# A block's transposes at the end of its group, its value products one group later: chunked attention feeding two feed-forward layers

## The chip, the cores and the metric

The kernel runs on one core of a Trainium2 chip. The metric is the device time of one execution in microseconds (us): the median of three runs of the kernel before was 1510.13 us (1508.39 to 1510.74). The engines are TensorE (PE; its weight loads are listed as PEld), VectorE (DVE), ScalarE (ACT), GpSimd (POOL) and SyncE (SP), which issues every DMA of this kernel. Nothing reorders the program: each engine's instructions stand in the order in which the kernel issues them.

## The reference, cut to what matters

```
# attention in chunks of 64 positions; q, k, v: (8, 8, 576, 64)
scores = 1/sqrt(64) * q_c @ k_c^T            # per chunk, 64 x 64
attn   = exp(scores - max) / (sum + 1e-9)
x      = attn @ v_c                          # then laid out as (4608 tokens, 512)
# first feed-forward layer, d_ff = 2048
h = x @ w_in ;  g = h * cos(h) ;  x = g @ w_out
# second layer, d_ff = 1024
out = (((x @ w1) * (x @ w2)) @ w3) @ w_out2
```

Every matrix product in fp32 is made of three products of high and low parts (`mm3`, L104 to L108), so operands are split into a high part (an ACT copy) and a low part (a DVE or POOL subtraction).

## The kernel before, in words

The 4608 tokens are 9 tiles of 512. The 2048 columns of the first layer are 8 groups of 256. The work of the first layer is done in two passes over the tiles: the first pass takes groups 0 to 4 of every tile (45 steps of the loop, `groups`, called groups below), the second pass groups 5 to 7. After that comes the second layer. This case is about the first pass.

Within a group the order is written out by hand as a string, one letter for one piece of work (`ORDER0`, `ORDER1P`, `ORDER1`, and the ones with an E at the end for the fifth group of a tile, which has no attention in it). Every engine gets its instructions in the order of the letters. The letters that matter here:

- `P`, `Q` (tiles 0 and 1) or `1`, `2`, `5`, `3` (later tiles): the input product x @ w_in into PSUM banks `ps_hh`. P's result is d, Q's is e. In the later tiles DVE adds the parts up (d at L489 and L501, e at L499 and L508).
- `a`, `c` (an ACT copy to integers, L547), `A`, `C` (DVE, L552), `b`, `d` (on ACT: Abs at L557, a table load, Sin at L558), `B`, `D` (DVE, L562): g = h * cos(h), the first letter of each pair for d and the second for e. In tiles 0 and 1 the PSUM bank of P is free again only when B has read it.
- `s`: the split of the previous group's g (ACT L570, POOL L571). `x`, `y`: the two halves of the previous group's output product g @ w_out into the four banks `acc` (12 matmuls each). At the first group of a tile `y` is followed by the copies of `acc` (L593, L595).
- `v` (tile 0): one step of the conversion of weights from HBM (`conv_tick`: ACT L124 and L177, DVE L125, L126, L132 and L199, and DMAs of SP). `l`, `m`, `h`, `r` and `M`, `H`, `R` (later tiles): the same kind of work, for weights that are staged in HBM.
- `o`, `S`, `T` (the fifth group): the split of the attention output xf into the operands X of the next tile (ACT L101, DVE L102).
- `q`: the next of the five attention steps of one block of 128 positions; there is one block in each of the first four groups of a tile, for the tile after. Step A is the scores (PE L361 into two banks `ps_s`; DVE L367 and L369; then the loads of q and k for a later block, SP L339 and L340). B is Exp (ACT L375, with a table load). E is the sums and the scaling (DVE L380 to L383, then POOL L384). C is the transposes (four matmuls, PE L391 into one bank `ps_at`, then the copy `pt` on ACT, L393). D is the values (32 small matmuls, PE L404 into two banks `ps_v`; the load of the next block's v, SP L345, into the one buffer `vt`; then two ACT copies into xf, L409).

The banks of `ps_s`, `ps_at` and `ps_v` are two that are given out in turn; `ex` and `pt` share two buffers; the banks `ps_hh` are two.

In the strings the five `q` of a group are A, B, E, C, D in this order. In tile 0 C stands behind `D` and one `v` ahead of the values, so the values end the group. In the later tiles C stands between `x` and `y`, and the values behind `y`.

Of the kernel before, what the change touches and what calls it, by code (L numbers as in the profile page):

```python
# [21 lines left out]
NJ = NT // P  # L22
# [4 lines left out]
FB2 = 8  # L27
# [6 lines left out]

START = "A0 A1 x B0 E0 B1 C0 x E1 A2 D0 C1 x B2 E2 A3 D1 C2 o o B3 E3 D2 C3 x D3 o o"

ORDER0 = "PsvaAqQvqcCqxybBdvDqvq"
ORDER0E = "PsvaAQvcCxybBodDoooL"
ORDER1P = "PsqMhQqqHaclAxqbCrRmBdyqDL"
ORDER1PE = "SPsQacATCoobBoxodoDyoo"  # L40
ORDER1 = "1s2qMh5qqHa3clAxqbCrRmBdyqDL"
ORDER1E = "S1s25a3cATCoobBoxodoDyoo"
ORDER2 = "1s2h5a3clAxbCrdByDm"
ORDER3 = "12sqhlrmq5a3cAbCdBDxy"
# [3 lines left out]
FOLD = 1  # L48
# [8 lines left out]
def chunk_attention_two_ffn(  # L57
# [38 lines left out]
    def f32(ap):  # L96
        return ap.bitcast(F32)
# [137 lines left out]
    def need(*keys):  # L235
        while not all(key in W for key in keys):
            assert (pump() if cat[3] == len(cq) else conv_tick()), keys
# [66 lines left out]
    def pump():  # L304

        n = 0
        while lq:
            key = lq[0]
            kept = (("w12", key[0][1] % FB2), key[1]) if key[0][0] == "w12" else key
            if kept not in staged or (kept != key or key[0][0] == "w12") and key[0][1] > unit[0] + AHEAD:  # L310
                break
            if key[1] == 3 and isinstance(key[0], tuple):
                if not free(s4s, 1):
                    break
                t = new_s4(key)
            elif free(slots, 1):
                t = new_w(key)
            else:
                break
            nc.sync.dma_start(out=f32(t), in_=staged[kept])  # L320
            lq.pop(0)
            n += 1
        return n
# [89 lines left out]
    def att_tok(step, early):  # L413
        (att_scores, att_softmax, att_scale, att_transpose, att_values)["ABECD".index(step[0])](int(step[1:]), early)
# [145 lines left out]
    def chain_g(i, h, which):  # L560
        t = rr[i, which]
        nc.vector.tensor_tensor(out=t, in0=t, in1=h, op=ALU.mult)  # L562
# [193 lines left out]
    with tc.manual_schedule():  # L756
# [17 lines left out]

        def order_of(i, nth, end):
            if i < GA:
                return ORDER0E if end else ORDER0
            if i < 2 * GA:
                return ORDER1PE if end else ORDER1P
            if i <= iA:  # L780
                return ORDER1E if end else ORDER1
            if i < iB:
                return ORDER2
            return (ORDER3X if nxt in xs else ORDER3E) if end else ORDER3B if nth else ORDER3

        steps = [s + str(j) for j in range(4, NJ) for s in "ABECD"]
        NG = len(groups)
        iA, iB = (NTILE - 1) * GA, NTILE * GA
        n_sums = 0
        fq = 0  # L790
        for i in range(NG):
            if i == GA:
                sq.extend(("wo2", j) for j in range(FB2))
                for g in range(GA, G1):
                    sq.extend((nm, 2 * g + e) for nm in ("in", "out") for e in range(2))
                    lq.extend((("in", g), p_) for p_ in range(4))
                    lq.extend(("out", 2 * g + e) for e in range(2))
                lq.extend(("wo2", j) for j in range(FB2))
                sq.extend(("w3", j) for j in range(N3))
                for f in range(FB2):  # L800
                    sq.extend((nm, f) for nm in ("w1", "w2"))
                    if N3 + f < 16:
                        sq.append(("w3", N3 + f))
                lq.extend((("w12", u), p_) for u in range(UNITS) for p_ in range(4))
                st_load()
            if i == iB + FOLD - 1:
                load_w3()
                load_w3()
            ps, n, g = groups[i]
            k_tile = (i - iB) // (G1 - GA)  # L810
            nxt = PASS2[k_tile + 1] if 0 <= k_tile < NTILE - 1 else None
            nth = (g, g - GA)[ps]
            end = g == (GA, G1)[ps] - 1

            def load_x(op):
                if op in pre:
                    X[op], pre[op] = pre[op], X[op]
                else:
                    nc.sync.dma_start(out=f32(X[op]), in_=xs[nxt][op])

            need(*((("in", g), p_) for p_ in range(2 if i < 2 * GA else 4)))
            z = Plain(("in", g)) if i < 2 * GA else Seven(
                ("in", g), (bank_h,) * 4, False, load_x if ps and end and nxt in xs else None)
            if i:
                need(*(("out", 2 * groups[i - 1][2] + e) for e in range(2)))
            n_q = n_o = 0
            for op in order_of(i, nth, end):
                if op == "s" and i:
                    split_g(i - 1)
                elif op == "x" and i:  # L830
                    x2_mm(i - 1, 0)
                elif op == "y" and i:
                    x2_mm(i - 1, 1)
                elif op == "v":
                    conv_tick()
                elif op == "L":
                    if n_sums < GA:
                        sum_load(n_sums)
                        n_sums += 1
                elif op == "M":  # L840
                    if loaded and i > GA + loaded[0][0]:
                        sum_make()
                elif op in "HR":
                    if sp:
                        {"H": sum_hi, "R": sum_lo}[op]()
                elif op == "l":
                    st_low()
                elif op == "m":
                    st_bits()
                elif op == "h":  # L850
                    st_hi()
                elif op == "r":
                    st_lo()
                elif op in "1253PQ":
                    getattr(z, "step" + op)()
                elif op in "ac":
                    chain_t(i, z.d if op == "a" else z.e, "ac".index(op))
                elif op in "AC":
                    chain_r(i, z.d if op == "A" else z.e, "AC".index(op))
                elif op in "bd":  # L860
                    chain_cos(i, "bd".index(op))
                elif op in "BD":
                    chain_g(i, z.d if op == "B" else z.e, "BD".index(op))
                elif op == "q":
                    if i < iA and nth < 4:
                        att_tok(steps[20 * n + 5 * nth + n_q], False)
                    elif i >= iB + FOLD and fq < 4 * FB2:
                        need(("w3", fq // 2), *(("wo2", j) for j in range(FB2)))
                        fold(fq // 4, fq % 4)
                        fq += 1  # L870
                        if fq == 4 * FB2:
                            load_wf(0)
                            load_wf(1)
                    n_q += 1
                elif op in "ST":
                    x_sums("ST".index(op))
                elif op == "o":
                    if i < GA and not n_o:
                        x_plain()
                    x_op((z.done if i < GA or i >= 2 * GA else OPS)[n_o], n + 1 if ps == 0 else None)  # L880
                    n_o += 1
            if i >= iA:
                pump()
            if n == (NTILE - 1, PASS2[-1])[ps]:
                done_with((("in", g), p_) for p_ in range(4))
            if ps == 1:
                if nth == 0 and nxt in xs:
                    if not pre:
                        xr = one.tile([P, CC, TT], F32R, tag="xf", name="xr")
                        pre.update((op, xr[:, 2 * j:2 * j + 2]) for j, op in enumerate(("B11", "B21")))  # L890
                    for op in pre:
                        nc.sync.dma_start(out=f32(pre[op]), in_=xs[nxt][op])
                if nth == 0 and nxt not in xs:
                    if pre:
                        pre.clear()
                        xf = one.tile([P, CC, TT], F32, tag="xf", name="xf")
                    nc.sync.dma_start(out=xf, in_=x2d[ALONE] if nxt is None else xd[nxt])
                if end:
                    for c in range(CC):
                        load_x2a(n, c)  # L900
        need(*(("out", 2 * G1 - 2 + e) for e in range(2)))
        assert fq == 4 * FB2 and sat[1] == len(sq) and not now
        split_g(NG - 1)
        for f in (4, 5, 6):
# [39 lines left out]
        j = FB2  # L944
# [75 lines left out]
```

## Time and profile before

| | |
|---|---|
| median of 3 runs | 1510.13 us (1508.39 to 1510.74) |
| profiled execution: time, and span of its instructions | 1515.81 us, 1514.0 us |
| PE busy | 1455.7 us, 96% of the span |
| DVE busy | 1099.8 us, 73% |
| ACT busy | 766.9 us, 51% |
| POOL busy | 262.0 us, 17% |
| first pass, tile 0 (groups 0 to 4) | about 34 to 115 us in the span |
| first pass, tile 1 | about 115 to 184 us |
| first pass, tiles 2 to 7 (attention still in them) | about 184 to 566 us |

A share is an average over stages; matmuls overlap, so a busy PE need not be at its peak. In the timelines below the number in front is the start in us from the beginning of the span, then the duration, the engine, the line, and in brackets the idle time ahead of the instruction with what ended it.

### The profile page before, as it was taken

The numbers are of one execution on the slowest core, as the hardware profiler recorded it, in microseconds if no ns is written. First come the engines' busy times: TensorE is split into PE (matmuls) and PEld (weight loads), VectorE is DVE, ScalarE is ACT, GpSimd is POOL, SyncE is SP. The second block draws the span as 40 slices with busy tenths as digits, with TensorE's granted clock in tenths as the row PEclk, the third lists the DMA queues.
The fourth block names the chain that finished last, engine by engine and source line by source line (L and its number), as shares of the span: only waits on it lengthen the run. The fifth ranks groups of instructions, "written<-read, shape, count | busy, mean of one in ns | idle before, by whom it ended". The sixth has DMA issues, their size and how long they took to land.

```text
span 1514.0 us, 26149 instructions
## 1 busy us (share of the span) xinstructions
PE 1455.7 (96%) x9996; PEld 1251.1 (83%) x9996; DVE 1099.8 (73%) x1844; ACT 766.9 (51%) x1317; POOL 262.0 (17%) x194
## 2 busy tenths in 40 slices
PE   4789999999999999999999989999999999999998
PEld 4678778888888888888888878898888888888886
DVE  6986798888988887767777777776665656656553
ACT  3777788888888876555555555321122013004002
POOL 0222222222222222222222112120100200200000
PEclk9999999999999999999999999999999999999999
DMA  7664555565665626998889774596434542641501
GB/s 235 204 210 133 188 173 204 188 228 166 227 218 165 229 88 248 363 328 299 309 308 326 252 282 127 196 367 238 152 140 154 190 153 90 228 157 59 210 33 56
DMA packets 122814, 307.39 MB, mean 203 GB/s; under 512 B 13633, under 2 KB 25665, under 8 KB 121537
## 3 DMA queue, kind: packets, MB, share of 16 engines
q1 hardware_dynamic: 122688, 305.71, 58.3%
q8 instruction: 79, 1.29, 0.4%
q14 instruction: 47, 0.38, 0.1%
HBM read 210.50 MB, written 95.16 MB: 202 GB/s over the span
## 4 chain that ended last, share of the span: by engine, by line
PE 65%; ACT 12%; DVE 12%; DMA 7%; issue 2%; POOL 1%; SPq 0%; DVEq 0%; ACTq 0%; POOLq 0%
PE ps_hh L106 9%; PE acc L107 8%; PE acc L106 8%; PE acc L108 8%; PE ps_hh L108 8%; PE ps_hh L107 8%; PE ps_aa L107 4%; PE ps_aa L106 4%; PE ps_aa L108 4%; ACT t L558 2%; DMA sd<-raw 2%; ACT L375 2%; ACT t L557 2%; ACT L558 1%; POOL ex L384 1%
## 5 line engine op out<-in xcount | busy, mean ns | idle before, releaser
L571 POOL TENSOR_TENSOR g<-t,g 128x512 fp32r<-128x512 f32 x144 | 196.2, 1384 | 591.6 <-ACT g L570 517.2
L106 PE MATMUL acc<-g,w 128*128 128x512 f32 x576 | 228.6, 397 | 0.0
L107 PE MATMUL acc<-g,w 128*128 128x512 f32 x576 | 227.1, 394 | 0.1
L108 PE MATMUL acc<-g,w 128*128 128x512 f32 x576 | 225.0, 391 | 0.0
L108 PE MATMUL ps_hh<-T,w 128*128 128x256 f32 (+1 forms) x616 | 182.2, 296 | 6.3 <-DVE w L199 6.2
L106 PE MATMUL ps_hh<-T,w 128*128 128x256 f32 (+1 forms) x616 | 185.3, 301 | 0.5 <-ACT x L481 0.5
L107 PE MATMUL ps_hh<-T,w 128*128 128x256 f32 (+1 forms) x616 | 181.8, 295 | 0.0
L108 PEld LDWEIGHTS acc<-g,w 128*128 128x128 f32 x576 | 108.5, 188 | 23.3
L107 PEld LDWEIGHTS acc<-g,w 128*128 128x128 f32 x576 | 108.9, 189 | 22.3 <-POOL g L571 3.0
L108 PEld LDWEIGHTS ps_hh<-T,w 128*128 128x128 f32 x616 | 118.6, 193 | 9.4 <-DVE w L199 6.9
L106 PE MATMUL ps_hh<-B,w 128*128 128x256 f32 (+1 forms) x396 | 120.4, 304 | 5.3 <-DVE t L562 3.3
L106 PEld LDWEIGHTS acc<-g,w 128*128 128x128 f32 x576 | 108.9, 189 | 19.7
L106 PEld LDWEIGHTS ps_hh<-T,w 128*128 128x128 f32 x616 | 118.6, 192 | 6.4 <-ACT x L481 0.9
L745 ACT ACTIVATE phl<-e 128x512 fp32r<-128x512 f32 x32 | 20.2, 633 | 201.5 <-DVE e L743 201.5
L107 PEld LDWEIGHTS ps_hh<-T,w 128*128 128x128 f32 x616 | 118.6, 193 | 3.2
L107 PE MATMUL ps_hh<-B,w 128*128 128x256 f32 (+1 forms) x396 | 116.6, 294 | 0.0
L108 PE MATMUL ps_hh<-B,w 128*128 128x256 f32 (+1 forms) x396 | 116.4, 294 | 0.0
L558 ACT ACTIVATE t<-t,half_pi 128x512 f32<-128x512 f32 x144 | 104.3, 724 | 4.0
L106 PE MATMUL acc<-wf,phl 128*128 128x512 f32 x252 | 98.2, 390 | 1.5 <-DVE o L688 1.5
L107 PE MATMUL acc<-wf,phl 128*128 128x512 f32 x252 | 98.1, 389 | 0.0
L108 PE MATMUL acc<-wf,phl 128*128 128x512 f32 x252 | 98.0, 389 | 0.0
L547 ACT ACTIVATE t<-d 128x512 int32<-128x512 f32 x62 | 38.9, 628 | 115.8 <-DVE d L501 115.8
(200 smaller groups left out, 3513.8 us busy)
## 6 DMA issues: line engine op xcount, KB each, us to landing
w<-sd SPq DMA_DIRECT2D x159, 512.0 KB, 5.6
sd<-raw SPq DMA_DIRECT2D x104, 256.0 KB, 4.5
s<-sd SPq DMA_DIRECT2D x43, 256.0 KB, 4.8
qk<-in_q_dram SPq DMA_DIRECT2D x36, 256.0 KB, 4.4
qk<-in_k_dram SPq DMA_DIRECT2D x36, 256.0 KB, 4.5
vt<-in_v_dram SPq DMA_DIRECT2D x72, 128.0 KB, 3.1
x2a<-x2o SPq DMA_DIRECT2D x36, 256.0 KB, 2.6
x2a<-x2a SPq DMA_DIRECT2D x36, 256.0 KB, 6.0
```

What stands on the lines that cost most here:

```text
L106: nc.tensor.matmul(ps, a[0], b[0], start=first, stop=False)
L107: nc.tensor.matmul(ps, a[0], b[1], start=False, stop=False)
L108: nc.tensor.matmul(ps, a[1], b[0], start=False, stop=last)
L375: nc.scalar.activation(ex, ex, AF.Exp, scale=SCALE)
L384: (nc.vector if early else nc.gpsimd).tensor_tensor(out=ex, in0=ex, in1=rc.unsqueeze(2).to_broadcast([P, 2 * HP, 64]), op=ALU.mult)
L547: nc.scalar.activation(t.bitcast(I32), h, AF.Copy, scale=INV2PI)
L557: nc.scalar.activation(t, t, AF.Abs)
L558: nc.scalar.activation(t, t, AF.Sin, scale=-TWO_PI, bias=half_pi)
L571: nc.gpsimd.tensor_tensor(out=lo, in0=r, in1=f32(hi), op=ALU.subtract)
L745: nc.scalar.activation(t[:, 0], e0, AF.Copy)
```

## The change

The five `q` are replaced by a digit for each step: `6` scores, `7` Exp, `8` sums and scaling, `9` transposes, `0` values, each with a counter of blocks of its own, so that a step can stand in another group than the one before it. Scores, Exp and scaling stay where they were.

- Tile 0: the transposes `9` stay behind `D`. The values `0` of a block move into the next group, between `x` and `y`. The first group has no values, and the fifth group (`ORDER0E`) has the last block's.
- Tiles 1 to 7: in the first three groups the transposes move from between `x` and `y` to the end, behind `y`. The values move to the next group, ahead of `x`. The fourth group has the third block's values ahead of `x`, its own transposes between `x` and `y`, and its own values behind `y`.

The load of v (L345) and the copies into xf (L409) move with the values, the copy `pt` (L393) with the transposes. Nothing is added or taken out, and no buffer or bank changes.

```
-ORDER0 = "PsvaAqQvqcCqxybBdvDqvq"
-ORDER0E = "PsvaAQvcCxybBodDoooL"
-ORDER1P = "PsqMhQqqHaclAxqbCrRmBdyqDL"
+ORDER0 = ("PsvaA6Qv7cC8xybBdvD9v",) + 3 * ("PsvaA6Qv7cC8x0ybBdvD9v",)
+ORDER0E = "PsvaAQvcCx0ybBodDoooL"
+ORDER1P = ("Ps6MhQ78HaclAxbCrRmBdy9DL",) + 2 * ("Ps6MhQ78HaclA0xbCrRmBdy9DL",) + ("Ps6MhQ78HaclA0x9bCrRmBdy0DL",)
 ORDER1PE = "SPsQacATCoobBoxodoDyoo"
-ORDER1 = "1s2qMh5qqHa3clAxqbCrRmBdyqDL"
+ORDER1 = ("1s26Mh578Ha3clAxbCrRmBdy9DL",) + 2 * ("1s26Mh578Ha3clA0xbCrRmBdy9DL",) + ("1s26Mh578Ha3clA0x9bCrRmBdy0DL",)
 ORDER1E = "S1s25a3cATCoobBoxodoDyoo"
...
             if i < GA:
-                return ORDER0E if end else ORDER0
+                return ORDER0E if end else ORDER0[nth]
             if i < 2 * GA:
-                return ORDER1PE if end else ORDER1P
+                return ORDER1PE if end else ORDER1P[nth]
             if i <= iA:
-                return ORDER1E if end else ORDER1
+                return "".join(o for o in ORDER1[0] if o not in "67890") if i >= iA and not end else ORDER1E if end else ORDER1[nth]
...
-        steps = [s + str(j) for j in range(4, NJ) for s in "ABECD"]
+        at_block = {s: 4 for s in "67890"}
...
+                elif op in at_block:
+                    att_tok("ABECD"["67890".index(op)] + str(at_block[op]), False)
+                    at_block[op] += 1
                 elif op == "q":
-                    if i < iA and nth < 4:
-                        att_tok(steps[20 * n + 5 * nth + n_q], False)
-                    elif i >= iB + FOLD and fq < 4 * FB2:
+                    if i >= iB + FOLD and fq < 4 * FB2:
```

## Rows read from the trace of the kernel before

**Rows 1.** Waits of PE, 44 to 560 us: total, times, longest
```profile
PE ps_at L391 <- POOL ex L384: 9.0, 13, 4.2
PE ps_hh L108 <- DVE w L199: 6.2, 2, 3.1
PE ps_hh L106 <- DVE t L562: 3.3, 4, 0.9
PE ps_v L404 <- ACT pt L393: 3.0, 4, 0.8
```

**Rows 2.** Busy time by stretch: length, engines, PE clock granted, DMA share
```profile
71.00:78.00 7.00, 7.00 (x76) 6.42 (x76) 6.93 (x15) 5.55 (x8) 0.00 (x0) 1.00 0.65 213
103.60:107.00 3.40, 3.06 (x14) 3.07 (x15) 1.48 (x3) 0.47 (x1) 0.00 (x0) 0.50 0.96 323
```

**Rows 3.** Timeline of PE, tile 0 and the start of tile 1
```profile
57.76 0.40 PE L106 MATMUL acc<-g,w 128*128 128x512 f32 x1
...
65.00 0.79 PE L404 MATMUL ps_v<-pt,vt 64*64 64x64 f32 x32 [0.78 <-ACT pt L393]
...
75.76 0.40 PE L106 MATMUL acc<-g,w 128*128 128x512 f32 x1
...
90.20 0.40 PE L106 MATMUL acc<-g,w 128*128 128x512 f32 x1
...
109.46 0.40 PE L106 MATMUL acc<-g,w 128*128 128x512 f32 x1
...
114.93 0.28 PE L106 MATMUL ps_hh<-B,w 128*128 128x256 f32 x1
...
117.89 0.69 PE L361 MATMUL ps_s<-qk 64*64 64x64 f32 x32
```

**Rows 4.** Timeline of ACT, tile 0
```profile
59.45 0.62 ACT L557 ACTIVATE t<-t 128x512 f32<-128x512 f32 x1
...
65.94 0.63 ACT L409 ACTIVATE xf<-ps_v 128x256 f32<-128x256 f32 x2
...
110.21 0.62 ACT L557 ACTIVATE t<-t 128x512 f32<-128x512 f32 x1
...
114.34 0.61 ACT L101 ACTIVATE B<-xf 128x512 fp32r<-128x512 f32 x1
```

**Rows 5.** Timeline of DVE, tile 0
```profile
62.22 0.64 DVE L562 TENSOR_TENSOR t<-t,ps_hh 128x512 f32<-128x512 f32 x1
62.78 1.29 DVE L132 CUSTOM_DVE_ANT_0 cw<-raw,cw 128x1024 uint16<-128x1024 uint16 x1
...
66.25 0.68 DVE L132 CUSTOM_DVE_ANT_0 cw<-raw,cw 128x1024 uint16<-128x1024 uint16 x1
...
79.20 0.69 DVE L562 TENSOR_TENSOR t<-t,ps_hh 128x512 f32<-128x512 f32 x1 [0.34 <-ACT t L558]
...
95.37 0.64 DVE L562 TENSOR_TENSOR t<-t,ps_hh 128x512 f32<-128x512 f32 x1
```

**Rows 6.** Timeline of ACT and DVE, first group of tile 1
```profile
124.88 0.60 ACT L393 ACTIVATE pt<-ps_at 128x512 f32<-128x512 f32 x1 [1.96 <-PE ps_at L391]
125.37 0.62 ACT L557 ACTIVATE t<-t 128x512 f32<-128x512 f32 x1
...
128.06 0.69 DVE L562 TENSOR_TENSOR t<-t,ps_hh 128x512 f32<-128x512 f32 x1 [3.10 <-ACT t L558]
```

**Rows 7.** Timeline of ACT and DVE, a group of tile 2
```profile
222.34 0.68 ACT L253 ACTIVATE raw<-raw 128x512 int32<-128x512 uint32 x1
223.09 0.60 ACT L393 ACTIVATE pt<-ps_at 128x512 f32<-128x512 f32 x1
223.59 0.62 ACT L557 ACTIVATE t<-t 128x512 f32<-128x512 f32 x1
...
228.87 0.69 DVE L489 TENSOR_TENSOR d<-x,ps_hh 128x512 f32<-128x512 f32 x1 [0.62 <-ACT g L570]
```

**Rows 8.** Transfers of `vt`, 183 to 560 us
```profile
DMA to landing us min/median/max: 2.6/3.1/5.3
```

More of the change, by code (lines that the diff above doesn't have):

```diff
@@ L901, in chunk_attention_two_ffn @@
         need(*(("out", 2 * G1 - 2 + e) for e in range(2)))
+        assert set(at_block.values()) == {NJ}
         assert fq == 4 * FB2 and sat[1] == len(sq) and not now
```

## The prediction

> **What bounds the kernel now.** I read the share of each engine first: TensorE is busy 96% of the span, so its waits look like the prize. Then its waits over the first pass [rows 1]: 9.0 us in 13 waits of the transposes for GpSimd's scaling, 3.0 us in 4 waits of the values for ScalarE's copy `pt`, 3.3 us of P for B, and 6.2 us in two waits of P for a converted weight (L199). The first two lie beside the steps that move. Then the busy time by stretch: in tile 0 VectorE is busy 6.93 of 7.00 us [rows 2], because it converts weights there. So TensorE's waits in tile 0 are a symptom, VectorE sets its length, and whatever makes VectorE idle there adds to the end. Last, the timelines of single groups, to see what stands in line behind each moved instruction on its own engine.
>
> 0.2% of 1510.13 is 3.0 us, about what a measurement of this kernel can tell from no change.
>
> **Tile 0: the copies into xf now stand ahead of the cosine.** Before, ScalarE goes from the copy to integers straight to Abs (`b`), and the two copies into xf come last in the group. Now they are issued between `c` and `b`, and they need the values, which TensorE takes up only after `x`. ScalarE's order is the program's, so Abs, the table load, Sin, and VectorE's B behind them wait for TensorE to finish `x` and the values. `x` is half of the 24 matmuls from 109.46 to 114.93, that is 2.74 us [rows 3]; from the start of the values (65.00) to the copies (65.94) it is 0.94 [rows 3, 4]; the pair of copies takes 0.63, and the next instruction starts 0.10 before the end of the one ahead, as at 223.59 [rows 7]: 0.53. Abs can start 2.74 + 0.94 + 0.53 = 4.21 us after Q's end. From Abs to B it is 62.22 - 59.45 = 2.77 [rows 4, 5].
>
> - Second group: Q ends at 57.76, so B at 64.74 instead of 62.22: 2.5 late. VectorE did something useful up to 62.22 (no idle is shown), so this is idle time. Given back: L132 took 1.29 behind B and takes 0.68 elsewhere [rows 5]; the late one no longer meets GpSimd's scaling, 0.6. The values no longer hold up P at the end of the first group: about 0.5, an estimate from their 0.79. Net 1.4.
> - Third group: Q ends at 75.76, B at 82.74 instead of 79.20, 3.5; with the 0.1 that is left of L132, 3.4. Q shifts with VectorE, since P waits for L199.
> - Fourth: Q ends at 90.20, B at 97.18 instead of 95.37, 1.8, less 0.6 for L132 as in the second (an estimate): 1.2.
> - Fifth: Q ends at 109.46, Abs at 113.67 instead of 110.21, 3.5 late, and the four splits of X for the next tile hang behind it. The last ACT part starts at 114.34 now, so at 117.8 then and ends at 118.4; its low part on VectorE follows that of the split before it, done about 119.4. The last quarter of P (2.96 us from 114.93 to 117.89) then ends at 120.3 instead of 117.9: 2.4 late, `x`, values and `y` included.
>
> Sum for tile 0: 1.4 + 3.4 + 1.2 + 2.4 = 8.4 us lost. The cover for a late B would be VectorE work that is ready ahead of it; there is none in program order. Bounds: 0 if such cover existed, and 2.5 + 3.5 + 1.8 + 3.5 = 11.3 with nothing given back.
>
> **Tensor clock.** TensorE waits for longer in tile 0. The two waits for L199, 3.1 us each [rows 1], lie in the third and in the fifth group. Behind the one in the fifth the clock was 0.50 from 103.6 to 107.0, that is 1.2 GHz; behind the other, from 71 to 78, it was 1.00 [rows 2]. One of two, so I count one more stretch of 3.4 us at half speed on the way to `x`, 1.7 us; bounds 0 and three of them, 5.1. The Trainium skill (TensorE: Matmul & The Clock Gate, Part 1) has the throttle as the default that activity lifts; by it all three longer waits would be followed by such a stretch, and the sum would be 3.4 higher. The trace agrees in one case and not in the other.
>
> **Tile 1.** In its first group `pt` waits 1.96 us for the transposes, with Abs right behind it [rows 6]: the same hold-up as above, and here the change removes it. With `pt` and its 0.49 gone from ahead of Abs, Abs moves up by 2.45 and B with it, B having waited 3.10. P loses its wait for B (3.3 in 4, 0.8 each [rows 1]) and the values ahead of it (0.79 at most): 1.4 gained, taking 0.6 for the values. In the next groups B follows VectorE's own work and P waits for B, so the period stays: no more gain. Bounds 0.8 to 2.5.
>
> **Tiles 2 to 7.** TensorE no longer waits for the scaling, but the chain that closes each group is ScalarE and VectorE: L253, `pt` and Abs follow each other at 222.34, 223.09, 223.59 without a gap to speak of; the only slack is the 0.62 us that L489 waits in the fourth group [rows 7]. The first group of a tile has no `pt` ahead of Abs, which can start 0.10 before L253 ends, at 222.92 instead of 223.59: 0.67. In the second and third the two copies stand where `pt` stood (0.53 for 0.50, less the 0.07 that `pt` waited); TensorE runs ahead and its scores wait for `pt` at the end of the group, in place of the transposes. In the fourth the slack of 0.62 goes, but xf and `pt` both stand ahead of Abs: about 0.57 back. Per tile 0.67 + 0.62 - 0.57 = 0.7. Tile 2 makes weight sums on VectorE, ahead of which the first 0.67 doesn't reach: 0.4, between 0.05 and 0.7. Sum 0.4 + 5 x 0.7 = 3.9. Bounds: 0, and 24 switches' worth of waits, the rest of the 9.0 and 3.0 [rows 1], about 6.
>
> **Queues.** In the fourth group the load of v is issued behind the first values and needed by the second: the transposes (0.4) and two halves of product lie between, 5.9 us, against a landing of 3.1 us and at most 5.3 [rows 8]. Nothing is counted; on a bad day some tenths a tile. On SP the load now stands ahead of the weight transfers of `r` and, in tile 0, of the later `v`, whose data come later than the values: nothing. GpSimd's scaling and splits keep their place: nothing. Banks: the values use the two that the next scores have left, read by L369 long before: nothing.
>
> **Sum.** 8.4 + 1.7 - 1.4 - 3.9 = 4.8 us more: 1515.81 becomes 1520.6 for an execution like the profiled one; that one is 5.7 over the median, so the forecast is 1510.1 + 4.8 = **1514.9 us**.
>
> **Rivals.**
> - *Half of tile 0's loss is made up* (no change to speak of): a VectorE instruction that meets GpSimd takes longer (1.29 for 0.68 [rows 5]); if VectorE's idle time pulls others apart from GpSimd's splits too, each of three late groups gets back 1 to 2 us. 8.4 - 4.5, no clock stretch, -5.3: 1508.7. For it: the row. Against: the splits on GpSimd hang on VectorE's D and shift along.
> - *Faster*: the late B is hidden, because TensorE or a DMA and not VectorE turns out to hold tile 0. Then the gains are left: -5.3, 1504.8. It decides from where tile 0's loss falls below 5.3 - 3.0 = 2.3 us. For it: P waits twice 3.1 us anyway. Against: what it waits for is VectorE.
> - *The waits pay in full*: 9.0 + 3.0, less the 4.2 of the first block, which nothing moves [rows 1]: 7.8 faster, 1502.3, if neither ScalarE's order in tile 0 nor the chain in later tiles counted. The queue of ScalarE stands against it: the Trainium skill (the same page, architectural detail in Part 1) calls ACT and DVE strict first-in first-out. If ScalarE could pass the waiting copies, the sum would be -5.3 or better; the idle 1.96 us of [rows 6], with Abs next, agrees with the page.
> - *Three clock stretches*: 3.4 more, 1518.3.
>
> **How the numbers follow.** The forecast 0.44, three stretches 0.12, half made up 0.27, faster with the loss hidden 0.12, waits in full 0.05. Slower by over 0.2%: 0.56; within: 0.27; faster: 0.17. The forecast's own range is 1512.5 to 1518. The range has to take in the middle case and part of the faster ones below, and the three stretches with 11.3 instead of 8.4 above: 1505 to 1521.
>
> **What would show it.** In tile 0, ScalarE idle ahead of the copies into xf (L409), released by `ps_v`, 2 to 3 us in three groups and in the fifth; VectorE's L562 (B) idle ahead by 2 to 3.5 us, released by Sin; tile 1 starting some 8 us later than 115. In tiles 2 to 7 no waits of `ps_at` for `ex`, but of `ps_s` for `pt` and tiles that are some 0.7 us shorter. I am wrong if B in tile 0 shows no such wait, or if the tiles after it are shorter by 1.5 us and more.

## The result: 11 us slower, and the profile after

| | before | changed |
|---|---|---|
| median, lowest to highest | 1510.43 us (1508.39 to 1511.39, 4 runs) | 1521.42 us (1519.38 to 1522.94, 4 runs) |
| ratio to before | 1 | 1.0066, 95% interval 1.0046 to 1.0086 |
| profiled execution: time, span | 1515.81 us, 1514.0 us | 1519.38 us, 1517.6 us |

By the ratio that is 0.66%, 10.0 us; the medians differ by 11.0. Forecast were 1514.9 us and a range from 1505 to 1521. The two profiled executions differ by only 3.6 us: the one of before lies 5.4 over its median and the changed one 2.0 under its own. So I compare stages, by the starts of the scores (L361) that open a group. Each column is one execution, so the rows carry some 2 us of chance: the same order of tile 0 as before took 76.6 us up to the scores of tile 1 in the trace of e1 below, and 78.8 here.

| scores that open | before | changed | difference |
|---|---|---|---|
| tile 0, first group | 39.07 | 36.44 | -2.63 |
| tile 0, second to fourth group | 54.16, 72.16, 86.59 | 53.91, 74.50, 95.05 | -0.25, +2.34, +8.46 |
| tile 1 | 117.89 | 130.03 | +12.14 |
| tile 2 | 187.42 | 198.35 | +10.93 |
| tile 3 | 252.54 | 262.93 | +10.39 |
| tile 7 | 505.09 | 513.93 | +8.84 |

Tile 0 loses 12.14 + 2.63 = 14.8 us, 2.4 of it ahead of the second group's scores, which is ahead of the first copies in their new place. Tile 1 gives 1.2 back, tile 2 0.5, and tiles 3 to 6 (10.39 - 8.84) / 4 = 0.39 each.

Waits of TensorE in the changed kernel, 44 to 570 us, the view of [rows 1] (us in total, times, longest):

```profile
PE ps_hh L108 <- DVE w L199: 10.4, 8, 2.0
PE ps_hh L106 <- ACT w L177: 5.2, 3, 1.7
PE ps_s L361 <- ACT pt L393: 4.3, 7, 1.2
PE ps_at L391 <- POOL ex L384: 4.2, 1, 4.2
PE ps_hh L106 <- DVE t L562: 2.6, 3, 1.0
PE ps_at L391 <- ACT xf L409: 1.9, 6, 0.4
```

The waits that lay beside the moved steps are gone: the transposes wait for GpSimd's scaling once, in the first group of tile 0, and the values no longer wait for `pt`. In their place P waits more often for converted weights (L199, and now ScalarE's L177), the scores wait for `pt`, and the transposes wait in six groups for the copies into xf.

Waits of ScalarE, and then of VectorE, 40 to 130 us of the changed kernel, and last the same line of VectorE from 40 to 119 us of the kernel before:

```profile
ACT t L547 <- PE ps_hh L108: 20.7, 9, 4.3
ACT xf L409 <- PE ps_v L404: 10.9, 4, 2.8
```

```profile
DVE t L562 <- ACT t L558: 17.5, 6, 4.2
DVE t L552 <- ACT t L547: 4.5, 4, 2.3
```

```profile
DVE t L562 <- ACT t L558: 1.8, 4, 0.6
```

The copies into xf wait four times, some 2.7 us each, and B (L562) waits behind them: 17.5 us in 6 times, where before it waited 1.8 in 4. That is 15.7 more; VectorE's other waits fall from 8.1 to 4.5, so in all it is idle 12.1 us longer, the greater part of what tile 0 loses. One group in the timelines of ScalarE and of VectorE (start, duration, engine and line, and in brackets the idle time ahead):

```profile
58.55 0.60 ACT L547 ACTIVATE t<-ps_hh 128x512 int32<-128x512 f32 x1 [0.84 <-PE ps_hh L108]
61.87 0.66 ACT L409 ACTIVATE xf<-ps_v 128x256 f32<-128x256 f32 x2 [2.73 <-PE ps_v L404]
62.42 0.63 ACT L557 ACTIVATE t<-t 128x512 f32<-128x512 f32 x1
63.07 1.28 ACT L558 ACT_TABLE_LOAD   x1
64.36 0.72 ACT L558 ACTIVATE t<-t,half_pi 128x512 f32<-128x512 f32 x1
...
66.27 0.61 ACT L177 ACTIVATE w<-cw 128x512 fp32r<-128x512 f32 x1
```

```profile
60.70 0.20 DVE L383 RECIPROCAL rc<-sm 128x8 f32<-128x8 f32 x1
65.12 0.69 DVE L562 TENSOR_TENSOR t<-t,ps_hh 128x512 f32<-128x512 f32 x1 [4.21 <-ACT t L558]
...
85.66 0.69 DVE L562 TENSOR_TENSOR t<-t,ps_hh 128x512 f32<-128x512 f32 x1 [4.21 <-ACT t L558]
...
106.22 0.69 DVE L562 TENSOR_TENSOR t<-t,ps_hh 128x512 f32<-128x512 f32 x1 [4.25 <-ACT t L558]
```

ScalarE finishes the copy to integers at 59.1 and stands still for 2.73 us, until TensorE has done `x` and the values; Abs, the table load and Sin follow, and VectorE, which before had work up to B [rows 5], is idle for 4.21. From B to B it takes 20.5 us now (65.12, 85.66, 106.22), against 17.0 and 16.2 before (62.22, 79.20, 95.37) [rows 5]. Sin of e is followed by the conversion copy L177, which P then waits for.

What TensorE does behind that wait, in its timeline:

```profile
66.93 0.39 PE L106 MATMUL ps_hh<-B,w 128*128 128x256 f32 x1 [1.72 <-ACT w L177]
...
68.13 0.39 PE L108 MATMUL ps_hh<-B,w 128*128 128x256 f32 x1 [0.69 <-DVE w L199]
...
72.07 0.58 PE L108 MATMUL ps_hh<-T,w 128*128 128x256 f32 x1 [2.01 <-DVE w L199]
72.45 0.41 PE L106 MATMUL ps_hh<-T,w 128*128 128x256 f32 x1
...
74.50 1.13 PE L361 MATMUL ps_s<-qk 64*64 64x64 f32 x32
```

And by stretch, in the view of [rows 2] (length, PE, PEld, DVE, ACT, POOL busy; granted clock; DMA share and GB/s):

```profile
65.00:69.40 4.40, 1.99 (x14) 1.57 (x13) 4.25 (x8) 4.37 (x9) 0.00 (x0) 1.00 0.44 134
69.40:76.20 6.80, 4.79 (x49) 4.15 (x48) 6.73 (x9) 3.31 (x7) 3.49 (x2) 0.50 0.53 157
76.20:85.00 8.80, 8.80 (x79) 7.50 (x79) 5.00 (x12) 5.23 (x9) 1.04 (x1) 1.00 0.60 194
85.00:89.90 4.90, 2.49 (x18) 1.95 (x17) 4.20 (x8) 4.87 (x9) 0.00 (x0) 1.00 0.43 133
89.90:96.70 6.80, 4.84 (x48) 4.21 (x48) 6.73 (x9) 3.25 (x7) 3.48 (x2) 0.50 0.49 152
...
106.00:110.40 4.40, 1.99 (x14) 1.54 (x13) 4.15 (x8) 4.37 (x9) 0.00 (x0) 1.00 0.16 60
110.40:117.20 6.80, 4.91 (x24) 4.62 (x23) 5.76 (x7) 2.39 (x5) 3.48 (x2) 0.50 0.00 1
```

In each of three groups TensorE works for 2.0 to 2.5 us in a stretch of 4.4 to 4.9, at 2.4 GHz, and then has 1.2 GHz for 6.8 us: scores that fall into it take 1.13 us instead of 0.69. There is a fourth slow stretch ahead of these, from the first group into the second, and it is twice as long:

```profile
42.10:55.80 13.70, 8.93 (x64) 7.84 (x65) 12.18 (x20) 9.10 (x17) 4.02 (x3) 0.50 0.57 191
```

The kernel before has 6.8 us there, shown further below. The mean granted clock of this execution is 0.988 over the span, that of the other three runs of the changed kernel 0.982 to 0.984, so they had more slow time than its trace shows.

In the fourth group of a later tile (tile 4) the timeline of TensorE, then those of ScalarE and VectorE, the view of [rows 7]:

```profile
367.28 0.69 PE L404 MATMUL ps_v<-pt,vt 64*64 64x64 f32 x32
...
371.27 0.63 PE L391 MATMUL ps_at<-ident,ex 128*128 128x128 f32 x4 [0.35 <-ACT xf L409]
```

```profile
370.77 0.64 ACT L409 ACTIVATE xf<-ps_v 128x256 f32<-128x256 f32 x2
371.94 0.60 ACT L393 ACTIVATE pt<-ps_at 128x512 f32<-128x512 f32 x1 [0.54 <-PE ps_at L391]
372.44 0.62 ACT L557 ACTIVATE t<-t 128x512 f32<-128x512 f32 x1
```

```profile
375.13 0.69 DVE L562 TENSOR_TENSOR t<-t,d 128x512 f32<-128x512 f32 x1 [1.25 <-ACT t L558]
```

The transposes take a bank that the values ahead of `x` have filled, so they wait for the copies out of it; `pt`, Abs and B wait behind them.

### The profile page after: what moved, and what is told of

Read it like the earlier page. It is cut to its first block, busy times and chain, and to the rows that moved or that the text cites. A ratio compares the mean times of both kernels' runs of the same rounds, so it can differ in the third digit from the quotient of the medians.

```text
span 1517.6 us, 26155 instructions
## 1 busy us (share of the span) xinstructions
PE 1456.9 (96%) x9996; PEld 1258.9 (83%) x9996; DVE 1096.3 (72%) x1844; ACT 764.4 (50%) x1317; POOL 264.0 (17%) x194
## 4 chain that ended last, share of the span: by engine, by line
PE 68%; DVE 14%; ACT 12%; DMA 3%; issue 2%; SPq 0%; POOL 0%; DVEq 0%; ACTq 0%; POOLq 0%
PE ps_hh L106 9%; PE ps_hh L108 9%; PE ps_hh L107 9%; PE acc L106 9%; PE acc L107 9%; PE acc L108 9%; PE ps_aa L106 4%; PE ps_aa L107 4%; PE ps_aa L108 4%; ACT t L558 2%; ACT t L557 2%; DVE t L562 1%; DVE e L508 1%; ACT L558 1%; ACT T L101 1%
```

## The experiments

**Which tiles.** Tile 0 in the order of before, the rest as changed; and the other way round.

```
e1:  ORDER0 = 4 * ("PsvaA6Qv7cC8xybBdvD9v0",);  ORDER0E = "PsvaAQvcCxybBodDoooL"
e2:  ORDER1P = 4 * ("Ps6MhQ78HaclAx9bCrRmBdy0DL",)
     ORDER1 = 4 * ("1s26Mh578Ha3clAx9bCrRmBdy0DL",)
```

> Tile 0 in its order of before, tiles 1 to 7 as changed. If the loss sits in tile 0 alone (ScalarE's copies into xf ahead of Abs, and what follows from it), the gain of tiles 1 to 7 is left, which the two traces put at 12.1 - 7.4 = 4.8 us between the scores at the start of tile 1 and the last ones: 1505 to 1507 us. If the moved transposes and values cost something in the later tiles that the scores' times don't show, it comes out at 1509 us or above.

> Tile 0 as changed, tiles 1 to 7 in their order of before. Tile 0 theory: 1521.4 + 4.8, so 1524 to 1527 us. Rival (loss spread over the pass): between 1511 and 1518 us.

e1: 1505.08 us (1501.3 to 1509.61, 12 runs), ratio 0.9969 (0.9954 to 0.9983). e2: 1525.16 us (1523.43 to 1528.86, 5 runs), ratio 1.0103 (1.0081 to 1.0124). Both as expected: tile 0 costs 0.0103 x 1510.4 = 15.6 us, tiles 1 to 7 bring 0.0031 x 1510.4 = 4.7, and the sum, +10.9, is the whole change.

**Is it the place of the copies into xf, or that of the values?** e3 leaves the values between `x` and `y` and issues tile 0's copies only behind Sin of e, by a new letter `k`. e4 has the values ahead of `x`, so that the copies don't have to wait for half an output product.

```
e3:  "...C8x0ybBdkvD9v"  and  "...Cx0ybBodkDoooL"
+        if late[0]:
+            held_copies.append(copies)
+        else:
+            copies()
...
+                elif op == "k":
+                    held_copies.pop()()
e4:  "...C80xybBdvD9v"   and  "...cC0xybBodDoooL"
```

> The changed kernel, with the values of tile 0 where the change puts them on TensorE, but their two copies into xf issued behind d (Sin of the second half) on ScalarE. ScalarE theory: Abs and B no longer wait for the values, tile 0 loses next to nothing, 1505 to 1509 us. Rival: the values between x and y, or TensorE's clock, are what costs; then it stays at 1517 to 1521 us.

> The changed kernel with the values of tile 0 ahead of x, as in the later tiles, the copies still ahead of Abs. ScalarE theory: what counts is how long the copies wait; now about 1.0 us behind Q's end instead of 3.7, so Abs can start 1.56 behind it and B 4.33, which is late by 0.9 in the third group, and not in the second and the fourth (B stood 4.46 and 5.17 behind Q's end before): 1506 to 1509 us. Rival, that copies ahead of Abs cost their 0.5 us and the values their 0.8 wherever they stand: 1514 to 1518.

e3: 1507.05 us (1503.57 to 1508.83, 12 runs), ratio 0.9976 (0.9962 to 0.9991). e4: 1507.06 us (1503.65 to 1509.76, 12 runs), ratio 0.9975 (0.9962 to 0.9988). Both 14 us below the changed kernel, and 2 above e1 (1 by the ratios, whose intervals overlap). So nearly all that tile 0 lost comes from the copies holding up ScalarE's line while they wait for the values: with the copies behind Sin the values may stay between `x` and `y`, and with the values early the copies may stay ahead of Abs. VectorE's timeline with the late copies (e3), then with the early values (e4):

```profile
79.52 0.20 DVE L383 RECIPROCAL rc<-sm 128x8 f32<-128x8 f32 x1
79.64 0.64 DVE L569 TENSOR_TENSOR t<-t,ps_hh 128x512 f32<-128x512 f32 x1
80.19 1.29 DVE L132 CUSTOM_DVE_ANT_0 cw<-raw,cw 128x1024 uint16<-128x1024 uint16 x1
```

```profile
79.77 0.69 DVE L562 TENSOR_TENSOR t<-t,ps_hh 128x512 f32<-128x512 f32 x1 [0.38 <-ACT t L558]
```

B (L569 in e3) follows the reciprocal without idle time in this group. From 40 to 130 us it waits 3.6 us for Sin in e3 and 5.9 in e4, instead of 17.5.

**What the clock costs.** The changed kernel, with transposes of the identity into the half of P's bank that the next matmuls overwrite, 8 ahead of the first half of P and 20 ahead of the second, in groups 2 to 5 of tile 0. Nothing reads them; they can only take TensorE's time, and keep it busy.

```
+FILL = (8, 20)
     w, ps = self.w[e], p[:, 256 * n:256 * n + 256]
+    for _ in range(self.fill[n]):
+        nc.tensor.transpose(p[:, 256 * n:256 * n + P], ident, ident)
```

> The changed kernel, with transposes of the identity into P's bank that nobody reads, 8 ahead of the first and 20 ahead of the second half of P in the groups two to five of tile 0, where TensorE otherwise waits. Clock theory: of tile 0's loss of 14.8 us some 5 are the three added stretches at 1.2 GHz (matmuls of P, scores and Q behind each wait 1.7 us longer in sum); without them 1515 to 1517 us. Rival: all of it is ScalarE's order, the slow matmuls lie beside VectorE's work: 1520 to 1523 us.

1514.38 us (1511.48 to 1517.07, 12 runs), ratio 1.0024 (1.001 to 1.0038), a little faster than I expected of the clock. By stretch, then the unread transposes among the groups of instructions from 34 to 130 us, and then B (L567 here) in VectorE's timeline:

```profile
64.00:72.00 8.00, 7.24 (x84) 6.43 (x82) 7.93 (x11) 5.61 (x11) 3.50 (x2) 1.00 0.53 166
72.00:80.00 8.00, 8.00 (x83) 6.87 (x76) 7.02 (x15) 5.06 (x10) 0.68 (x1) 1.00 0.75 228
80.00:88.00 8.00, 6.66 (x49) 5.71 (x47) 6.09 (x10) 7.92 (x13) 1.96 (x2) 1.00 0.54 152
```

```profile
L523 PE MATMUL ps_hh<-ident 128*128 128x128 f32 x112 | 14.2, 280 | 2.0 <-DVE t L567 2.0
```

```profile
63.05 0.69 DVE L567 TENSOR_TENSOR t<-t,ps_hh 128x512 f32<-128x512 f32 x1 [3.73 <-ACT t L563]
...
81.84 0.69 DVE L567 TENSOR_TENSOR t<-t,ps_hh 128x512 f32<-128x512 f32 x1 [2.69 <-ACT t L563]
```

TensorE does 14.2 us more work, and the kernel gets (1.0066 - 1.0024) x 1510.4 = 6.3 us faster (7.0 by the medians). The clock is 1.00 from 56 us on, and from B to B it is 18.8 us instead of 20.5. The long stretch ahead of that is shorter too: the granted clock is 0.89 from 34 to 48 us and 0.98 from 48 to 56, which is some 3.4 us at half speed instead of 13.7. In the two traces tile 0 is 7.0 us shorter: 1.0 up to the second group's scores, and 6.0 behind them, where the three stretches were. So the slow stretches together cost 6.3 us at least; what the transposes themselves lengthen is not in it. B still waits 2.7 and more for Sin: that part of the loss is untouched.

**The fourth group's bank.** e1, and in tiles 2 to 7 the fourth group's transposes go to one of the two banks that P and Q use (`ps_hh`; the transposes' tile in it is called `ps_ah`).

```
-  att_tok(..., False)
+  att_tok(..., op == "9" and i >= 2 * GA and nth == 3)
```

> As e1 (tile 0 in its order of before), with the transposes of the fourth group of tiles 2 to 7 in a bank of ps_h instead of one of the two that the values of the third block still hold. Theory: those transposes wait for the copies into xf, 0.35 us in each of six tiles, and pt and Abs behind them 0.54; taking the bank away gives 0.3 to 0.5 us a tile, 2 to 3 us under e1. Rival: the wait is covered by a later one of the chain, no difference from e1 (within 1 us).

1502.26 us (1499.84 to 1506.34, 6 runs), ratio 0.9941 (0.9924 to 0.9957): 2.8 us under e1 (4.2 by the ratios, whose intervals just overlap), and faster than both kernels. Of TensorE's waits from 180 to 570 us, first e1 and then e6:

```profile
PE ps_s L361 <- ACT pt L393: 4.3, 7, 1.2
PE ps_at L391 <- ACT xf L409: 1.9, 6, 0.4
PE ps_hh L106 <- ACT x L481: 0.2, 1, 0.2
```

```profile
PE ps_s L361 <- ACT pt L393: 4.3, 7, 1.2
PE ps_hh L106 <- ACT x L481: 1.3, 2, 1.1
```

The transposes no longer wait; P waits 1.3 us where it waited 0.2. From the scores that open tile 3 to those of tile 4 it is 63.15 us before, 62.74 in e1, and 62.27 here: 0.47 a tile, 2.8 in six.

**Do the repairs add up?** e7 is e6 with the unread transposes; e8 has the late copies of e3, the other bank, and the unread transposes.

> The kernel with tile 0 in the old order and the fourth group's transposes in another bank, plus the 28 unread transposes a group in groups 2 to 5 of tile 0. In its profile without them the clock is 0.94 and 0.85 in the stretches 80 to 88 and 88 to 96 us, about 3.4 us at 1.2 GHz while VectorE is busy for 7.93 and 6.17 of 8.00. If a stretch costs about 2 us as in the changed kernel (6.4 to 7 us for three of 6.8), about 1 to 2 us come back: 1500.3 to 1501.5 against 1502.3 without. If VectorE hides the slower matmuls here, the unread transposes bring nothing or cost their own time: 1502 to 1504.

> The changed order in all tiles, with tile 0's copies into xf behind Sin of e, the fourth group's transposes in another bank, and the 28 unread transposes a group in groups 2 to 5 of tile 0: the three repairs together. If they are independent: 1507.1 with late copies, less 2.8 for the bank, less up to 2 for a stretch of about 5 us at 1.2 GHz that the profile with late copies has between 80 and 96 us: 1502.3 to 1504.3, no better than tile 0 in the old order with the other bank (1502.3). If late values of their own hold up the next group's P, it stays at 1505 or more.

e7: 1505.55 us (1503.76 to 1508.7, 12 runs), ratio 0.9971 (0.9958 to 0.9985), against 0.9941 without: 3.3 us slower by the medians, more than I expected of the rival. Its clock is 1.00 from 56 us on, where e6 has 0.94 and 0.85 from 80 to 96 us; here that was not worth its price. In its timeline of TensorE, ahead of P's second half:

```profile
86.90 2.34 PE L523 MATMUL ps_hh<-ident 128*128 128x128 f32 x20
```

The scores of tile 0 and the first of tile 1 start at 37.28, 56.29, 73.45, 90.61 and 118.99 in e7, and at 37.40, 53.45, 69.42, 87.04 and 114.05 in e6: e7 loses 3.0 us up to the second group, where both still have a slow stretch (the granted clock from 48 to 56 us is 0.72 in e7 and 0.69 in e6), then 1.2, gains 0.5, and loses 1.4. The transposes, 14.6 us of TensorE's time in tile 0, are longer than what TensorE waits for the weights in e6 (4.7 us in 2 waits). That this is why they don't pay here is argued, and not shown.

e8: 1502.95 us (1500.48 to 1503.74, 6 runs), ratio 0.9951 (0.9932 to 0.997): as expected for independent repairs, and no better than e6, which moves nothing in tile 0. There is no run of e8 without the transposes, so what they cost or bring in it is open.

## Why the prediction was right in direction and short in size

- **"The copies into xf now stand ahead of the cosine": right.** From Q's end to B the text had 6.98 us (4.21 + 2.77); it measured 6.83 (58.29 to 65.12), with ScalarE released by `ps_v` and B by Sin, as listed. e3 and e4 show that this is the cause of nearly all of tile 0's loss: they take away 14.4 of the 16.3 us between the medians of the changed kernel and e1. The term was 8.4 us; what is left of 15.6 without the clock's 6.3 to 7.0 is 8.6 to 9.3, an estimate, as the kernel before has slow stretches too and the transposes of e5 a price. Its parts can't be checked group by group: between the scores of the second and the third group 2.6 us were lost and up to those of the fourth 6.1, where 1.4 and 3.4 stood, but against the trace of e1, which has the same old order, it is 4.5 and 2.9, and all contain slow matmuls. Ahead of the second group's scores, where the text had 0.5 gained, 2.4 were lost (1.5 against e1). e3 and e4 have the same program up to there and take 1.0 less: the long slow stretch, and not a copy.
- **"Tensor clock", one more stretch of 3.4 us, 1.7: this is the step that failed.** Where the kernel before has one stretch of 3.4 us there were three, one a group, 6.8 us long each, and the one ahead of them was 13.7 us long instead of 6.8. Taking away the three and most of that one gave 6.3 to 7.0 us, about four times the term; the bound was 5.1. How much of it the kernel before pays as well, for its own two stretches, no run separates, so whether the added ones alone pass the bound is open. The number of three was the rival's; I had taken the 3.4 us of [rows 2]. The kernel before has one of 6.8 as well, earlier in tile 0, behind a stretch in which TensorE works half the time, as in the changed kernel; the argument did not use it. In the view of stretches:

```profile
40.00:45.60 5.60, 2.84 (x24) 2.63 (x22) 5.50 (x13) 4.18 (x7) 0.00 (x0) 1.00 0.53 174
45.60:52.40 6.80, 4.60 (x47) 4.08 (x48) 6.40 (x12) 6.56 (x14) 2.01 (x2) 0.50 0.53 155
```

I had looked only behind the two waits for L199 that were there, and counted how many of them would recur. But the late Sin makes a wait of its own ahead of P's first half: L177 stands behind Sin of e on ScalarE, and P waits for it, 1.72 us in three groups. The text had P waiting for VectorE alone. Which of the waits brings the slow stretch no run tells.
- **Why the slow matmuls are paid for.** The text took VectorE as what sets tile 0 throughout. Once B waits for ScalarE and ScalarE for `x`, tile 0 is a circle: B lets P start, P and Q lead to `x`, `x` to the copies, and these to Sin and B. TensorE's time is on it. That is argued from the timelines; what e5 shows is that 2.4 GHz shortens each turn by 1.7 us although VectorE has no less work. In the three stretches TensorE is busy for 14.5 us; twice the clock can bring back half of that at most, 7.3 (an estimate), and 6.0 came.
- **Tile 1, 1.4: right**, 1.2.
- **Tiles 2 to 7, 3.9: the right sign, about half the size in tiles 3 to 7.** 0.4 a tile and not 0.7 (tile 2: 0.5, and 0.4 stood). The step is "Banks: ... nothing". It looked at the scores, and overlooked that in the fourth group the values ahead of `x` and the transposes behind it come one after the other and share a bank. e6 gives that back, 0.47 a tile. 4.7 us for tiles 1 to 7 came out against 5.3.
- **"Queues": right.** The load of v landed in 2.6, 2.8 and 4.1 us (shortest, median, longest), against [rows 8], and nothing waits for it.
- **The rivals.** *Three clock stretches* came closest, 1518.3, and was still 3.1 short; it had 3.4 us for the length of a stretch. The Trainium skill (TensorE: Matmul & The Clock Gate, Part 1) has the throttle as the default state that activity lifts; the trace agrees here in three groups of three, and e5 agrees from the other side. *Half made up* and *faster* fell: the late B is idle time in all four groups, 4.0 to 4.25 us each. *The waits pay in full* fell with them: ScalarE let nothing pass the waiting copies, 10.9 us in four groups.

## What to carry to other kernels

Before an instruction is moved, read who stands behind it on its own engine and what it waits for: a pair of copies of 0.6 us, early by a few letters in the program, cost some 15 us in four groups, because Sin stood behind them and they waited for 2.7 us in each. Cost a new wait of TensorE twice, as the wait and as what its clock does afterwards: here the second was 6 to 7 of the 15 us. Moving a matmul to another time moves its PSUM bank too: list who takes that bank next.

## What the runs showed of the hardware that I had not expected

- Matmuls that nobody reads can make a kernel faster: 112 transposes, 14.2 us of TensorE's time, took 6.3 us off the changed kernel, with the granted clock at 1.00 where it had been 0.50. The same ones cost 3.3 us in e7, where TensorE waited less for weights.
- The slow stretches were 6.8 us long behind waits of much the same pattern (1.72, 0.69, with two matmuls between), but [rows 2] has one of 3.4 us at a single wait of 3.1, and none behind the other wait of that length. At the wait of 4.2 us in the first group, which the kernels share, it was 6.8 us before, 13.7 in the changed kernel and some 3.4 in e5. No run here says what sets the length.
